# Moving unit 1.3's bonus work, a weight load and one r product in a hand-ordered RWKV-6 plus SwiGLU kernel

## The chip, the cores and the metric

The kernel runs on one core of a Trainium2 chip. The core has five instruction streams that run beside each other: TensorE (PE in the profile, with its weight loads listed as PEld), VectorE (DVE), ScalarE (ACT), GpSimd (POOL) and SyncE (SP), which here only issues DMAs. Each stream works through its instructions in the order in which the program issued them; a semaphore makes one wait for another. The metric is the device time of one execution in microseconds (us), lower is better.

## The reference

The first half is an RWKV-6 attention over 4 batches, 8 heads, 768 positions and a head size of 48; the second half a SwiGLU feed-forward on its output, 3072 tokens of width 384, hidden width 1536.

```
for t in range(S):
    cur = einsum('bhd,bhe->bhde', u[None] * kt, vt)
    y[:, :, t] = einsum('bhd,bhde->bhe', rt, state + cur)
    state = wt[:, :, :, None] * state + einsum('bhd,bhe->bhde', kt, vt)
x = y.transpose(0, 2, 1, 3).reshape(B * S, H * D)
xn = x / sqrt(mean(x * x) + 1e-6) * rms_g
g, val = xn @ w_gate, xn @ w_val
out = (g * sigmoid(g) * val) @ w_out
```

Inputs and output are float32; the kernel multiplies in bfloat16.

## The kernel before

**Tiling.** The sequence is cut into six blocks of 128 positions. A unit n.j is block n of batch j, so there are 24 units, and each has the same steps. Positions lie on the partitions. Inside a block the recurrence becomes matrix products: the decays are logged (ln), summed along the block by a triangular matmul (cs_mm) and exponentiated (exp_r, exp_k); r_mul and k_mul scale r and k with them; rk_pe and rk_tr bring both to head-major form (by TensorE transposes and a ScalarE copy in blocks 0 and 1, by a DMA transpose from block 2 on); q_mm gives the 128x128 products per head, q_mask_e and, after q_copy_o, q_mask_o keep their lower triangles (even and odd heads); y_mm multiplies them with v, and with the state carried from the block before; st_mm and st_new make the next state.

**The bonus term.** The diagonal, r·(u·k) times v, is a separate strand: bonus_mul (two GpSimd products, lines 467 and 468, into one of three buffers "ruk"), bonus_sum (a VectorE sum, line 472), bonus_v (a GpSimd product with v, line 477), and x_add on VectorE, which joins it to y. In block 0, x_pe joins it by a TensorE matmul instead.

**The feed-forward.** x_sq, x_rstd, xn_mul, xn_pe and xn_out normalise x, transpose it and apply the gain. When the four units of a block are there, gate_mm and val_mm run for twelve pieces f of the hidden width, each three matmuls of 128x512 (line 626); silu and h_mul join the two; o_mm sums the twelve pieces into one output tile (line 672), o_out copies it and out_dma writes it. The feed-forward of block n runs between the attention steps of block n+1.

**Weights.** W_gate and W_val come in two parts: load_gv.0.0 and load_gv.0.1 bring the first 512 columns of gate and val, load_gv.1.0 and load_gv.1.1 the remaining 1024, and load_wo brings W_out in three thirds (four of its twelve pieces each, so that the ninth matmul of an o_mm is the first to read the last third). All of them are issued from GpSimd's queue (lines 351 and 357) and converted to bfloat16 on the way; r, k, v and w come through SP's queue (lines 248 and 261).

**Order.** The order of all steps is written out as one list of 1086 names, ORDER; the last loop of the program calls them one after the other, and each engine keeps that order among its own instructions. Nothing else schedules. k_mul is on VectorE in blocks 0 and 1 and on GpSimd after that; in block 1 its inputs, and those of r_mul, are both in SBUF (tiles er and ek), and in block 0 one is in PSUM.

**PSUM.** Eight banks are in three rings: a (two, gate and cs_r), b (two, val and cs_k) and q (four, all else). `psum` gives the bank whose last use lies furthest back in ORDER; the profile names them ps_au, ps_av, ps_bu, ps_bv, ps_qu, ps_qv, ps_qx, ps_qz. Matmuls named warm, ahead of the feed-forward's start, have no reader.

```
rings = {"a": [[-2, 0], [-2, 1]], "b": [[-2, 0], [-2, 1]], "q": [[-2, 0], [-2, 1], [-2, 2], [-2, 3]]}
for step in ORDER.split():
    fn, n, j = step.split(".")
    fns[fn](int(n), int(j))
    at[0] += 1
```

Of the kernel before, what the change touches and what calls it, by code (L numbers as in the profile page):

```python
# [51 lines left out]
x_rstd.1.0 q_mask_e.1.3 q_copy_o.1.2 val_mm.0.8 silu.0.8 val_mm.0.11 y_mm.1.1 silu.0.10 q_mask_e.1.2 bonus_sum.1.2
q_mask_o.1.3 h_mul.0.8 x_add.1.1 y_mm.1.3 st_mm.1.2 load_v.2.1 ln.2.0 st_mm.1.3 q_mask_o.1.2 val_mm.0.10 y_mm.1.2
x_sq.1.1 xn_mul.1.0 bonus_v.1.2 cs_mm.2.0 x_add.1.3 x_sq.1.3 st_new.1.2 h_mul.0.11 ln.2.1 h_mul.0.10 x_add.1.2
cs_add.2.0 o_mm.0.0 o_out.0.0 x_rstd.1.1 x_sq.1.2 xn_pe.1.0 xn_out.1.0 xn_mul.1.1 exp_r.2.0 st_new.1.3 cs_mm.2.1
cs_add.2.1 x_rstd.1.2 load_r.2.3 r_mul.2.0 o_mm.0.2 xn_pe.1.1 xn_mul.1.2 xn_pe.1.2 x_rstd.1.3 o_mm.0.1 xn_mul.1.3
# [5 lines left out]
gate_mm.1.5 cast_v.2.0 k_mul.2.3 silu.1.5 rk_tr.2.2 val_mm.1.5 load_w.3.3 o_out.0.2 h_mul.1.1 gate_mm.1.3 gate_mm.1.0
val_mm.1.0 h_mul.1.5 o_out.0.3 silu.1.0 val_mm.1.6 q_mm.2.0 load_v.2.3 q_copy_o.2.0 silu.1.3 q_mask_o.2.0 gate_mm.1.2
st_mm.2.0 h_mul.1.0 val_mm.1.3 rk_tr.2.3 h_mul.1.6 load_w.3.1 load_w.3.0 gate_mm.1.10 val_mm.1.2 load_k.3.1
q_mask_e.2.1 silu.1.2 st_new.2.0 gate_mm.1.4 q_copy_o.2.1 cast_v.2.2 silu.1.4 q_mask_o.2.1 h_mul.1.3 q_mask_e.2.0
y_mm.2.1 y_mm.2.0 h_mul.1.2 st_mm.2.2 bonus_v.2.0 silu.1.10 x_add.2.1 x_add.2.0 gate_mm.1.9 val_mm.1.4 x_sq.2.1
gate_mm.1.8 val_mm.1.9 bonus_mul.2.3 st_new.2.2 out_dma.0.1 x_sq.2.0 h_mul.1.4 load_v.3.2 x_rstd.2.0 silu.1.9 silu.1.8
q_mm.2.2 bonus_sum.2.2 q_copy_o.2.2 h_mul.1.9 gate_mm.1.11 q_copy_o.2.3 out_dma.0.2 load_w.3.2 cast_v.2.3 bonus_v.2.2
bonus_sum.2.3 q_mask_o.2.3 st_mm.2.3 load_k.3.0 q_mask_o.2.2 q_mask_e.2.3 val_mm.1.11 q_mask_e.2.2 val_mm.1.10
bonus_v.2.3 y_mm.2.3 silu.1.11 y_mm.2.2 ln.3.0 h_mul.1.11 h_mul.1.10 x_rstd.2.1 x_add.2.2 ln.3.1 val_mm.1.8 ln.3.3  # L70
h_mul.1.8 cs_mm.3.0 load_r.3.0 x_sq.2.2 xn_mul.2.0 cast_v.3.2 cs_add.3.0 x_add.2.3 exp_k.3.0 x_sq.2.3 o_mm.1.0
cs_mm.3.1 xn_pe.2.0 exp_r.3.0 ln.3.2 x_rstd.2.2 o_mm.1.1 st_new.2.3 load_r.3.1 out_dma.0.3 w_tot.3.0 r_mul.3.0
xn_mul.2.1 k_mul.3.0 xn_mul.2.2 cs_add.3.1 exp_k.3.1 xn_pe.2.2 cs_mm.3.3 x_rstd.2.3 o_out.1.0 exp_r.3.1 bonus_mul.3.1
xn_out.2.2 xn_mul.2.3 o_mm.1.3 w_tot.3.1 xn_pe.2.3 o_out.1.1 cs_add.3.3 r_mul.3.1 load_k.3.2 load_r.3.3 xn_pe.2.1
xn_out.2.0 exp_r.3.3 exp_k.3.3 cs_mm.3.2 xn_out.2.3 o_mm.1.2 load_r.3.2 k_mul.3.1 w_tot.3.3 rk_tr.3.0 r_mul.3.3
cs_add.3.2 out_dma.1.0 xn_out.2.1 load_v.3.0 exp_r.3.2 gate_mm.2.5 exp_k.3.2 r_mul.3.2 w_tot.3.2 val_mm.2.0 gate_mm.2.0
bonus_mul.3.0 bonus_mul.3.2 k_mul.3.2 o_out.1.3 bonus_sum.3.0 silu.2.5 rk_tr.3.1 load_k.3.3 o_out.1.2 q_mm.3.0 silu.2.0
q_mask_e.3.0 val_mm.2.1 bonus_v.3.0 h_mul.2.0 gate_mm.2.1 load_w.4.1 load_v.3.1 load_k.4.3 st_mm.3.2 k_mul.3.3
q_copy_o.3.0 silu.2.1 rk_tr.3.2 load_v.4.0 rk_tr.3.3 val_mm.2.5 gate_mm.2.11 load_k.4.0 bonus_sum.3.1 cast_v.3.0
out_dma.1.1 load_v.3.3 load_w.5.2 q_mask_e.3.1 q_copy_o.3.1 gate_mm.2.2 silu.2.11 h_mul.2.5 val_mm.2.2 h_mul.2.1  # L80
load_w.4.0 gate_mm.2.3 load_v.4.1 silu.2.2 q_mask_o.3.0 cast_v.3.1 load_r.4.1 bonus_sum.3.2 h_mul.2.2 bonus_v.3.1
# [643 lines left out]
```

## Time and profile before

| what | value |
|---|---|
| time, median of 3 runs | 200.89 us (199.61, 200.89, 200.95) |
| profiled execution | span 199.4 us from first to last instruction; no other time of it is recorded |
| TensorE busy | 194.7 us |
| VectorE busy | 151.5 us |
| ScalarE busy | 137.1 us |
| GpSimd busy | 125.7 us |
| granted TensorE clock | 1.00 throughout |
| DMA traffic | 32.41 MB, 163 GB/s over the span |

A timeline row reads: start and length in us, engine, source line, operation, output tile <- input tiles, shape, count, and in brackets how long the engine had been idle and what released it. A TensorE row of several matmuls ends with the modelled end of the last one, so rows overlap. A DMA row gives the issue, the size and the us from issue to landing. The queue named q0 is GpSimd's, q1 is SP's.

### The profile page before, as it was taken

Reading aid. Unit: us, or ns where it says so; the run is one execution under the profiler, and the core shown is the slowest. Engines: PE = TensorE matmul, PEld = TensorE weight load, DVE = VectorE, ACT = ScalarE, POOL = GpSimd, SP = SyncE. Lnnn points to the kernel's source line nnn. Section 1 sums busy time; section 2 is a strip of 40 time slices with the busy share of each in tenths; the row PEclk is TensorE's granted clock in tenths of the full one; section 3 lists DMA queues with packets and bytes.
Section 4 is the critical chain, followed back from the end, with each engine's and each line's share of the span. In section 5 each row is a group of like instructions: output and inputs, shape, how many; then the busy total and the mean of one; then the engine's idle time right before and its main releaser. Section 6 shows DMA issues by size and latency. Waiting matters only on the chain.

```text
span 199.4 us, 4410 instructions
## 1 busy us (share of the span) xinstructions
PE 194.7 (98%) x1577; PEld 115.6 (58%) x1577; DVE 151.5 (76%) x290; ACT 137.1 (69%) x279; POOL 125.7 (63%) x184
## 2 busy tenths in 40 slices
...
GB/s 147 265 229 191 169 206 208 201 207 191 203 173 212 204 191 227 217 191 191 177 175 226 214 203 215 179 174 139 122 190 219 0 24 60 2 116 82 0 59 100
DMA packets 121566, 32.41 MB, mean 163 GB/s; under 512 B 116420, under 2 KB 120392, under 8 KB 121544
## 3 DMA queue, kind: packets, MB, share of 16 engines
...
q8 instruction: 12, 0.20, 0.4%
...
## 4 chain that ended last, share of the span: by engine, by line
PE 88%; DMA 5%; DVE 2%; POOL 2%; issue 1%; ACT 0%
PE ps_bu L626 12%; PE ps_av L626 12%; PE ps_au L626 11%; PE ps_bv L626 11%; PE ps_qu L672 7%; PE ps_qz L672 7%; DMA wg_sb<-in_moe_w_gate_dram 5%; PE ps_qx L672 5%; PE ps_qv L672 5%; PE ps_qz L502 1%; PE ps_qx L552 1%; PE ps_qv L502 1%; PE ps_qv L333 1%; PE ps_qu L285 1%; PE ps_qu L502 1%
## 5 line engine op out<-in xcount | busy, mean ns | idle before, releaser
L672 PEld LDWEIGHTS <-ht 128*128 128x128 bf16 x300 | 28.2, 98 | 16.6
L626 PEld LDWEIGHTS <-wg_sb 128*128 128x128 bf16 x216 | 23.1, 114 | 19.8 <-DMA wg_sb<-in_moe_w_gate_dram 0.9
L626 PEld LDWEIGHTS <-wv_sb 128*128 128x128 bf16 x216 | 23.0, 114 | 18.3
L658 DVE TENSOR_TENSOR ht<-ps_bv,sg 128x512 bf16<-128x512 f32 x35 | 24.0, 687 | 10.2 <-PE ps_bv L626 9.1
L658 DVE TENSOR_TENSOR ht<-ps_bu,sg 128x512 bf16<-128x512 f32 x37 | 25.4, 687 | 6.9 <-PE ps_bu L626 5.8
L235 ACT ACTIVATE sg<-ps_av 128x512 bf16<-128x512 f32 x37 | 22.0, 596 | 12.2 <-PE ps_av L626 11.6
L626 PE MATMUL ps_av<-xnt,wg_sb 128*128 128x512 bf16 x111 | 30.1, 380 | 0.0
L626 PE MATMUL ps_bu<-xnt,wv_sb 128*128 128x512 bf16 x111 | 30.1, 380 | 0.0
L626 PE MATMUL ps_au<-xnt,wg_sb 128*128 128x512 bf16 x105 | 28.5, 380 | 0.5 <-DMA wg_sb<-in_moe_w_gate_dram 0.5
L626 PE MATMUL ps_bv<-xnt,wv_sb 128*128 128x512 bf16 x105 | 28.5, 380 | 0.0
L235 ACT ACTIVATE sg<-ps_au 128x512 bf16<-128x512 f32 x35 | 21.0, 600 | 10.5 <-PE ps_au L626 8.7
L467 POOL TENSOR_TENSOR ruk<-rt,kt 128x384 f32<-128x384 f32 x24 | 24.0, 1001 | 6.1 <-DMA kt<-in_k_dram 5.2
L468 POOL TENSOR_TENSOR ruk<-ruk,u_bc 128x384 f32<-128x384 f32 x24 | 24.7, 1030 | 1.9
L520 POOL TENSOR_SCALAR_AFFINE_SELECT qts<-qts 128x512 bf16<-128x512 bf16 x20 | 12.8, 650 | 15.1 <-ACT qts L513 14.6
L477 POOL TENSOR_TENSOR ydiag<-vt,diag 128x384 f32<-128x384 f32 x24 | 20.2, 843 | 1.7 <-DVE diag L472 1.6
L461 POOL TENSOR_TENSOR rk<-kt,ek 128x384 bf16<-128x384 f32 x16 | 15.9, 1004 | 2.3 <-ACT ek L235 2.3
L672 PE MATMUL ps_qu<-wo_sb,ht 128*128 128x384 bf16 (+1 forms) x96 | 15.0, 306 | 0.0
L672 PE MATMUL ps_qz<-wo_sb,ht 128*128 128x384 bf16 x84 | 14.8, 326 | 0.0
L233 ACT ACT_TABLE_LOAD x10 | 12.8, 1283 | 1.8 <-PEq L709 1.6
L472 DVE TENSOR_REDUCE diag<-ruk 128x8 f32<-128x384 f32 x24 | 13.0, 543 | 0.2 <-POOL ruk L468 0.2
L235 ACT ACTIVATE lw<-wt 128x384 bf16<-128x384 f32 (+1 forms) x20 | 11.1, 577 | 2.6 <-DMA wt<-in_w_dram 2.6
L585 ACT ACTIVATE xn<-xb,rstd 128x384 bf16<-128x384 f32 x20 | 11.8, 603 | 0.8 <-POOL rstd L580 0.7
...
## 6 DMA issues: line engine op xcount, KB each, us to landing
rt<-in_r_dram SPq DMA_DIRECT2D x24, 192.0 KB, 4.0
kt<-in_k_dram SPq DMA_DIRECT2D x24, 192.0 KB, 4.2
vt<-in_v_dram SPq DMA_DIRECT2D x24, 192.0 KB, 4.0
out_dram<-ob SPq DMA_DIRECT2D x23, 192.0 KB, 2.3
wt<-in_w_dram SPq DMA_DIRECT2D x16, 192.0 KB, 4.0
wt<-in_w_dram SPq DMA_DIRECT2D x4, 384.0 KB, 4.4
wo_sb<-in_moe_w_out_dram POOLq DMA_DIRECT2D x3, 384.0 KB, 7.0
...
```

Of the source, the lines that this page charges most:

```text
L233: nc.scalar.preload_act_table_set(table_name)
L235: return nc.scalar.activation(**kw).ins
L461: eng.tensor_tensor(out=rk[:, n % 2, j, 1, :, 0:D], in0=inp["k", n, j], in1=bank["cs_k", n, j][:, 0:DM].rearrange("p (h d) -> p h d", h=H) ...
L467: nc.gpsimd.tensor_tensor(out=ruk[n, j], in0=inp["r", n, j], in1=inp["k", n, j], op=ALU.mult)
L468: nc.gpsimd.tensor_tensor(out=ruk[n, j], in0=ruk[n, j], in1=u_bc, op=ALU.mult)
L472: nc.vector.tensor_reduce(out=diag[n, j].rearrange("p h o -> p (h o)"), in_=ruk[n, j], axis=mybir.AxisListType.X, op=ALU.add)
L477: nc.gpsimd.tensor_tensor(out=ydiag[n, j], in0=inp["v", n, j], in1=diag[n, j].to_broadcast([128, H, D]), op=ALU.mult)
L520: nc.gpsimd.affine_select(out=qts[n, j][:, 1], in_=qts[n, j][:, 1], compare_op=ALU.is_gt, fill=0.0, base=0, pattern=[[0, NP], [1, 128]], c ...
L585: nc.scalar.activation(out=xn, in_=xb[n, j], func=AF.Copy, scale=rstd[n, j][:, 1, c:c + 1])
L626: nc.tensor.matmul(ps[:, cols], lhsT=units(ws, c, f), rhs=xnt[n][:, c, cols], start=(first and c == 0), stop=(c == KC - 1))
L658: nc.vector.tensor_tensor(out=ht[n][:, f, :], in0=bank.pop(("v", n, f)), in1=bank.pop(("sg", n, f)), op=ALU.mult)
L672: nc.tensor.matmul(ps[:, cols], lhsT=ht[n][:, f, b * L:(b + 1) * L], rhs=wo_sb[:, f, cols], start=(f == 0), stop=(f == FC - 1))
```

## The change

Only ORDER is changed; all 1086 steps are still there. Engine by engine, the moves are:

- GpSimd: load_gv.0.1 goes ahead of bonus_v.0.3 (it stood behind bonus_mul.1.0, directly ahead of load_gv.1.0); bonus_mul.1.3 goes behind q_mask_o.1.0 (it stood behind load_gv.1.1).
- VectorE: bonus_sum.0.3 goes ahead of q_mask_o.0.2; r_mul.1.1 goes behind xn_out.0.3 (it stood ahead of st_new.0.0 and r_mul.1.0), and st_new.0.3 goes there too, behind it; k_mul.1.3 goes behind q_mask_e.1.1, and bonus_sum.1.3 behind h_mul.0.6; w_tot.2.3 and r_mul.2.3 change places.
- TensorE: rk_pe.1.3 goes behind gate_mm.0.5 (it stood ahead of val_mm.0.6); rk_pe.1.2 goes ahead of gate_mm.0.4.
- SP: load_v.1.2 goes ahead of load_v.1.1.
- ScalarE: nothing moves.

With the order, `psum` gives ps_qu and ps_qv the other way round to a part of the tiles of ring q.

```diff
-load_r.1.3 load_k.1.3 load_r.1.2 load_k.1.2 r_mul.0.1 load_v.1.0 load_v.1.1 load_v.1.2 exp_k.0.0 bonus_mul.0.1
+load_r.1.3 load_k.1.3 load_r.1.2 load_k.1.2 r_mul.0.1 load_v.1.0 load_v.1.2 load_v.1.1 exp_k.0.0 bonus_mul.0.1
...
-q_mask_o.0.0 rk_pe.0.3 q_mask_e.0.0 q_mm.0.2 x_pe.0.0 x_sq.0.1 cast_v.0.3 rk_tr.0.3 q_mask_o.0.2 load_gv.0.0
-bonus_sum.0.3 q_mask_e.0.2 cs_mm.1.1 x_rstd.0.1 q_mm.0.3 warm.17.0 bonus_v.0.2 q_mask_o.0.3 y_mm.0.0 warm.25.0
-exp_r.1.1 load_w.2.3 x_pe.0.2 load_k.2.1 cast_v.0.2 bonus_v.0.3 warm.20.0 x_sq.0.0 y_mm.0.2 st_mm.0.0 warm.6.0
+q_mask_o.0.0 rk_pe.0.3 q_mask_e.0.0 q_mm.0.2 x_pe.0.0 x_sq.0.1 cast_v.0.3 rk_tr.0.3 bonus_sum.0.3 q_mask_o.0.2
+load_gv.0.0 q_mask_e.0.2 cs_mm.1.1 x_rstd.0.1 q_mm.0.3 warm.17.0 bonus_v.0.2 q_mask_o.0.3 y_mm.0.0 warm.25.0 exp_r.1.1
+load_w.2.3 x_pe.0.2 load_k.2.1 cast_v.0.2 load_gv.0.1 bonus_v.0.3 warm.20.0 x_sq.0.0 y_mm.0.2 st_mm.0.0 warm.6.0
...
-y_mm.0.3 exp_k.1.1 cs_mm.1.3 k_mul.1.0 xn_pe.0.1 warm.0.0 bonus_mul.1.0 load_gv.0.1 load_gv.1.0 x_rstd.0.2 warm.30.0
-x_sq.0.3 xn_mul.0.2 r_mul.1.1 st_new.0.0 xn_pe.0.0 r_mul.1.0 warm.14.0 x_rstd.0.3 warm.28.0 warm.33.0 xn_pe.0.2
-xn_out.0.1 bonus_mul.1.1 warm.11.0 xn_mul.0.3 exp_k.1.3 xn_out.0.0 st_mm.0.3 xn_out.0.2 st_mm.0.2 xn_pe.0.3 exp_r.1.3
-st_new.0.3 cs_mm.1.2 rk_pe.1.0 xn_out.0.3 k_mul.1.1 st_mm.0.1 st_new.0.1 k_mul.1.3 gate_mm.0.0 exp_r.1.2 bonus_sum.1.0
-exp_k.1.2 rk_pe.1.1 gate_mm.0.3 rk_tr.1.0 val_mm.0.0 silu.0.0 bonus_sum.1.1 load_gv.1.1 load_r.2.2 bonus_mul.1.3
-silu.0.3 val_mm.0.2 rk_tr.1.1 h_mul.0.0 gate_mm.0.2 st_new.0.2 silu.0.2 gate_mm.0.1 bonus_sum.1.3 val_mm.0.3
-gate_mm.0.9 silu.0.1 h_mul.0.2 val_mm.0.1 gate_mm.0.6 silu.0.9 r_mul.1.3 h_mul.0.3 q_mm.1.0 h_mul.0.1 silu.0.6
-q_mask_e.1.0 q_copy_o.1.0 q_mask_o.1.0 gate_mm.0.11 gate_mm.0.7 q_copy_o.1.1 silu.0.7 rk_pe.1.3 q_mask_e.1.1
-q_mask_o.1.1 r_mul.1.2 bonus_v.1.0 val_mm.0.6 val_mm.0.7 cast_v.1.0 k_mul.1.2 rk_tr.1.3 gate_mm.0.5 h_mul.0.6 y_mm.1.0
-load_wo.0.0 val_mm.0.9 silu.0.11 bonus_v.1.1 cast_v.1.2 load_wo.1.0 st_mm.1.0 cast_v.1.1 gate_mm.0.4 rk_pe.1.2
+y_mm.0.3 exp_k.1.1 cs_mm.1.3 k_mul.1.0 xn_pe.0.1 warm.0.0 bonus_mul.1.0 load_gv.1.0 x_rstd.0.2 warm.30.0 x_sq.0.3
+xn_mul.0.2 r_mul.1.0 st_new.0.0 xn_pe.0.0 warm.14.0 x_rstd.0.3 warm.28.0 warm.33.0 xn_pe.0.2 xn_out.0.1 bonus_mul.1.1
+warm.11.0 xn_mul.0.3 exp_k.1.3 xn_out.0.0 st_mm.0.3 xn_out.0.2 st_mm.0.2 xn_pe.0.3 exp_r.1.3 cs_mm.1.2 rk_pe.1.0
+xn_out.0.3 r_mul.1.1 st_new.0.3 k_mul.1.1 st_mm.0.1 st_new.0.1 gate_mm.0.0 exp_r.1.2 bonus_sum.1.0 exp_k.1.2 rk_pe.1.1
+gate_mm.0.3 rk_tr.1.0 val_mm.0.0 silu.0.0 bonus_sum.1.1 load_gv.1.1 load_r.2.2 silu.0.3 val_mm.0.2 rk_tr.1.1 h_mul.0.0
+gate_mm.0.2 st_new.0.2 silu.0.2 gate_mm.0.1 val_mm.0.3 gate_mm.0.9 silu.0.1 h_mul.0.2 val_mm.0.1 gate_mm.0.6 silu.0.9
+r_mul.1.3 h_mul.0.3 q_mm.1.0 h_mul.0.1 silu.0.6 q_mask_e.1.0 q_copy_o.1.0 q_mask_o.1.0 bonus_mul.1.3 gate_mm.0.11
+gate_mm.0.7 q_copy_o.1.1 silu.0.7 q_mask_e.1.1 k_mul.1.3 q_mask_o.1.1 r_mul.1.2 bonus_v.1.0 val_mm.0.6 val_mm.0.7
+k_mul.1.2 cast_v.1.0 gate_mm.0.5 rk_pe.1.3 rk_tr.1.3 h_mul.0.6 bonus_sum.1.3 y_mm.1.0 load_wo.0.0 val_mm.0.9 silu.0.11
+bonus_v.1.1 cast_v.1.2 load_wo.1.0 st_mm.1.0 cast_v.1.1 rk_pe.1.2 gate_mm.0.4 h_mul.0.7 st_mm.1.1 silu.0.5 val_mm.0.5
...
-val_mm.1.7 exp_k.2.2 load_k.2.3 st_mm.2.1 rk_tr.2.0 bonus_sum.2.0 r_mul.2.3 w_tot.2.3 gate_mm.1.1 load_v.2.2 st_new.2.1
+st_mm.2.1 rk_tr.2.0 bonus_sum.2.0 w_tot.2.3 r_mul.2.3 gate_mm.1.1 load_v.2.2 st_new.2.1 k_mul.2.2 silu.1.7
```

138 lines of the change are left out of this document (69 added, 69 removed).

## The prediction

> **What bounds the kernel now.** I read the page first, then the chain of waits in order of time, then each engine's timeline from 20 to 55 us, where the moved steps lie. Of the page, the busy shares and the head of the chain; of the stretches, one row (busy us and count of PE, PEld, DVE, ACT, POOL; clock; DMA share; GB/s):
>
> ```profile
> PE 194.7 (98%) x1577; PEld 115.6 (58%) x1577; DVE 151.5 (76%) x290; ACT 137.1 (69%) x279; POOL 125.7 (63%) x184
> PE 88%; DMA 5%; DVE 2%; POOL 2%; issue 1%; ACT 0%
> 37.00:198.00 161.00, 159.42 (x1291) 94.61 (x1291) 124.33 (x236) 109.43 (x223) 101.57 (x149) 1.00 0.73 155
> ```
>
> TensorE is the bound. From 37.0 us it is busy for 159.42 us, so up to 196.4 us without a hole, at clock 1.00. A new wait of TensorE behind 37 us is therefore paid in full, and a gain has to be made ahead of it. The DMA part of the chain, and TensorE's timeline ahead of 37 us:
>
> ```profile
> 25.85 0.61 POOL wv_sb L351
> ...
> 26.60 10.27 DMA wg_sb<-in_moe_w_gate_dram
> ```
> ```profile
> 28.87 0.32 PE L374 MATMUL ps_qx<-still 128*128 128x384 bf16 x1
> 29.35 0.33 PE L530 MATMUL ps_qu<-vb,rk 128*128 128x96 bf16 x4 [0.16 <-DVE xnt L607]
> 29.82 0.33 PE L596 MATMUL ps_qv<-ident,xn 128*128 128x128 bf16 x3
> ...
> 31.95 0.61 PE L484 MATMUL ps_qv<-ident,rk 128*128 128x128 bf16 x8
> ...
> 34.99 0.81 PE L626 MATMUL ps_av<-xnt,wg_sb 128*128 128x512 bf16 x3
> 35.63 0.81 PE L626 MATMUL ps_bv<-xnt,wv_sb 128*128 128x512 bf16 x3
> 36.92 0.84 PE L626 MATMUL ps_au<-xnt,wg_sb 128*128 128x512 bf16 x3 [0.47 <-DMA wg_sb<-in_moe_w_gate_dram]
> ```
>
> Three holes are there to be won. A 128x384 matmul lets the next one start 0.16 us after its own start (the twelve of 52.66, quoted below: 2.11 less the last one's 0.33, over eleven), so the successor of 28.87 could have started at 29.03; it started at 29.35, held by xn_out of unit 0.1 on VectorE. A group of three takes 0.65 us to the next one's start (34.99 to 35.63), so the one at 36.92 could have started at 36.28, had the second gate block been there: 0.64 us lost. And xn_pe of unit 0.3 (29.82) lost 0.13.
>
> **The change, front part.** VectorE and GpSimd around it (idle ahead of a row in brackets):
>
> ```profile
> 24.91 1.35 DVE L455 TENSOR_TENSOR rk<-rt,er 128x384 bf16<-128x384 f32 x1
> ...
> 26.66 2.18 DVE L455 TENSOR_TENSOR rk<-rt,er 128x384 bf16<-128x384 f32 x1
> 28.75 0.55 DVE L607 TENSOR_TENSOR xnt<-ps_qu,gT 128x384 bf16<-128x384 bf16 x1
> ...
> 30.61 0.54 DVE L607 TENSOR_TENSOR xnt<-ps_qv,gT 128x384 bf16<-128x384 bf16 x1
> 31.08 0.82 DVE L461 TENSOR_TENSOR rk<-kt,ek 128x384 bf16<-128x384 f32 x1
> ...
> 36.73 0.55 DVE L455 TENSOR_TENSOR rk<-rt,er 128x384 bf16<-128x384 f32 x1
> ```
> ```profile
> 22.65 0.83 POOL L477 TENSOR_TENSOR ydiag<-vt,diag 128x384 f32<-128x384 f32 x1 [1.02 <-DVE diag L472]
> ...
> 27.40 1.01 POOL L467 TENSOR_TENSOR ruk<-rt,kt 128x384 f32<-128x384 f32 x1
> ...
> 31.55 1.21 POOL L468 TENSOR_TENSOR ruk<-ruk,u_bc 128x384 f32<-128x384 f32 x1
> ```
>
> (1) load_gv.0.1 goes ahead of bonus_v.0.3, into the 1.02 us that GpSimd idled at 22.65; its issue was worth 0.75 (25.85 to 26.60), so it is hidden. bonus_sum.0.3, one step earlier on VectorE, keeps bonus_v.0.3 at 22.4 to 22.65. load_gv.1.0 loses that issue ahead of it and goes out at 25.3 to 25.85. With its 10.27 us it lands at 35.6 to 36.1; with the second block queued directly behind the first, earlier still. TensorE will want it at 36.1 (below), so the 0.64 us go.
>
> (2) An r_mul with both inputs in SBUF takes 0.55 us beside an idle GpSimd (36.73) and 2.18 us beside a busy one (26.66); it ended at 28.84, 0.43 after the GpSimd product of 27.40. The k_mul at 31.08 took 0.82, and the GpSimd product beside it, 31.55, 1.21 for about 1.0. So each holds the other. The Trainium skill, "SBUF — State Buffer", section "Who interferes with whom", says that of a VectorE instruction with two SBUF inputs and a GpSimd instruction that reads SBUF, the later one blocks until the first ends; the trace agrees, and by a split of bandwidth in its place the lock terms below would be near nothing.
>
> With r_mul.1.1 gone from here, xn_out.0.1 waits for TensorE's transposes alone. st_mm.0.3 starts at 29.03, xn_pe.0.3 at 29.37, xn_out.0.3 at 29.75 for 30.61. Behind it now stand r_mul.1.1, st_new.0.3 and k_mul.1.1, at a step of 0.47 each (30.61 to 31.08): k_mul.1.1 starts at 31.15 and ends at 31.7 beside an idle GpSimd, since bonus_mul.1.3 is gone from there. rk_pe.1.1 needs it and starts at 31.75 for 31.95. TensorE has a new stall of about 0.25 there; 0.20 is kept. From there 0.20 + 0.64 = **0.84 us earlier at 36.9**, and no more, since k_mul.1.1 is the limit.
>
> (3) What pays for the earlier weights are SP's loads. Queue packets and MB in 23 to 25 us (weights moving), 25.6 to 27.9 (none moving), 32 to 39 (the large block); ahead of them the landings of k of 1.1 (issued 20.09) and r of 1.3 (20.78):
>
> ```profile
> kt<-in_k_dram SPq DMA_DIRECT2D x1, 192.0 KB, 6.3
> ```
> ```profile
> rt<-in_r_dram SPq DMA_DIRECT2D x1, 192.0 KB, 6.5
> ```
> ```profile
> q0 software_dynamic: 301, 0.31, 90.6%
> q1 hardware_dynamic: 345, 0.07, 28.3%
> ```
> ```profile
> q1 hardware_dynamic: 2772, 0.52, 115.6%
> ```
> ```profile
> q0 software_dynamic: 647, 1.29, 97.2%
> q1 hardware_dynamic: 642, 0.12, 15.9%
> ```
>
> SP's queue moves 226 KB per us alone, 35 beside the small blocks and 17 beside the large one. The free stretch at 25.6 now belongs to the second block. k of 1.1 landed at 26.4; between nothing and 190 KB of it were left at 25.4, so it lands between 26.4 and some 33. I take 45 KB and 27.7, as its neighbour r of 1.3 landed at 27.3, 0.9 us (192 KB) later. bonus_mul.1.1 then starts at 27.7 for 27.40, which costs nothing; beyond 31 it would hold k_mul.1.1. r of 1.3 has 192 KB more to wait for. At 155 KB per us (0.31 MB in 2 us) the second block takes 2.5 us, at 184 the large one 4.3, and beside them SP moves 88 and 73 of the 237 KB. Some 75 are left at 32.2, so r lands between 33.5 (a gap in the weights' queue) and 37.5 (none). r_mul.1.3 wants it at 36.3, and h_mul.0.3 stands behind it, whose buffer the next silu on ScalarE uses, ahead of q_copy_o.1.0. Between 0 and 0.65 us; I take 0.25. That leaves **0.6 us won** where unit 1's masks begin.
>
> The Trainium skill, "DMA: Bandwidth & Descriptors", section "Queues, rings and completion order", says that each DMA engine goes round its queues packet by packet. The trace agrees: 647 packets against 642, at ten times the bytes. By equal bytes SP would not starve, and the 0.25 would be nothing.
>
> **The change, unit 1.3.** bonus_mul.1.3 leaves 30.46, behind which GpSimd idled for 7.48 us, and goes behind the first affine_select of 40.23. GpSimd, then the wait of TensorE for what it issues:
>
> ```profile
> 40.23 1.54 POOL L520 TENSOR_SCALAR_AFFINE_SELECT qts<-qts 128x512 bf16<-128x512 bf16 x2 [7.48 <-ACT qts L513]
> 41.75 1.12 POOL L477 TENSOR_TENSOR ydiag<-vt,diag 128x384 f32<-128x384 f32 x1
> 42.82 0.61 POOL L357 DMA_DIRECT2D wo_sb<-in_moe_w_out_dram  x1
> ...
> 44.85 1.01 POOL L467 TENSOR_TENSOR ruk<-rt,kt 128x384 f32<-128x384 f32 x1
> ...
> 46.88 0.59 POOL L357 DMA_DIRECT2D wo_sb<-in_moe_w_out_dram  x1
> ...
> 49.24 1.22 POOL L520 TENSOR_SCALAR_AFFINE_SELECT qts<-qts 128x512 bf16<-128x512 bf16 x2
> ```
> ```profile
> wo_sb<-in_moe_w_out_dram POOLq DMA_DIRECT2D x1, 384.0 KB, 7.0
> ```
> ```profile
> DMA to landing us min/median/max: 6.3/7.0/7.5
> ```
> ```profile
> 50.65 0.33 PE L549 MATMUL ps_qx<-st,rkT 128*128 128x96 bf16 x4
> ...
> 52.66 2.11 PE L672 MATMUL ps_qx<-wo_sb,ht 128*128 128x384 bf16 x12
> ```
>
> GpSimd has no bracket from 40.23 to 50.4: it is full there. A pair of products costs 44.85 to 46.88, 2.03 us. To this comes the lock: k_mul.1.3, r_mul.1.2 and k_mul.1.2 on VectorE now fall on four GpSimd instructions. Before, two such meetings stretched a pair of selects from 1.22 (49.24) to 1.54 and a product from 0.83 (22.65) to 1.12, 0.6 us together; three to four meetings give 0.9 to 1.2. I take 0.4 more (ends 0 and 0.9). So everything behind it on GpSimd is 2.43 us late, 1.83 with the 0.6 won.
>
> Who waits: the select for unit 1.3 ended at 49.87 (half of the pair at 49.24) and y_mm.1.3 read it at 50.65, 0.78 of slack; 1.05 us are paid there. The last third of W_out was issued at 46.88 and landed 7.0 later, at 53.88. o_mm.0.0's twelve matmuls start 0.16 apart, and the ninth, the first to read that third, at 53.95: slack 0.07. It is issued at 48.7, lands at 55.7, and the ninth matmul is 1.76 us late. The 1.05 are part of these, not added.
>
> VectorE hides beneath. It ran h_mul.0.6 for val_mm.0.9's bank:
>
> ```profile
> 42.23 0.69 DVE L658 TENSOR_TENSOR ht<-ps_bv,sg 128x512 bf16<-128x512 f32 x1
> ```
> ```profile
> 43.62 0.82 PE L626 MATMUL ps_bv<-xnt,wv_sb 128*128 128x512 bf16 x3
> ```
>
> With k_mul.1.3 and three lock waits ahead of it h_mul.0.6 ends near 44.3 for 42.92, and val_mm.0.9 would be 0.7 late, less than what GpSimd costs. rk_pe.1.3 goes behind three groups (1.95 us), and its copy on ScalarE stands ahead of silu.0.11; gate_mm.0.4, which takes that silu's bank, comes behind the delayed val_mm.0.9, which covers it; uncovered it would cost some 0.5, inside the same wait. Nothing: the order of load_v.1.2 and load_v.1.1 (their casts stand in that order), w_tot.2.3 ahead of r_mul.2.3 (both run anyway), and the exchanged PSUM names u and v (same ring, same number in use).
>
> **Sum.** −0.84 + 0.25 + 2.03 + 0.40 − 0.07 = **+1.8 us**, carried to the end: a span of 201.2 for 199.4. The profiled execution's own time is known by its span alone; the runs were 199.61 to 200.95, median 200.89, 1.5 over the span. I forecast 200.89 + 1.8 = 202.7.
>
> **Rivals.** (A) Faster: the front gain stays and GpSimd's delay is not felt, 200.89 − 0.84 = 200.05. It decides at the ninth matmul of o_mm.0.0: W_out's last third must land by 53.1, so the delay would have to vanish in the queue. For it: the thirds landed 6.3 to 7.5 us after their issues, the first (42.82) by 49.1 and the last by 53.9, 4.8 apart where the issues are 4.06 apart, so the last waits in the queue. Against: the first is issued behind bonus_mul.1.3 too. 0.11. (B) W_out catches up on an emptier queue, and y_mm.1.3 alone decides: −0.59 + 2.43 − 0.78 = +1.06, 201.95. 0.22. (C) The loads starve more: r of 1.3 at 37.5 and k of 1.1 near 31, so that the masks start 0.6 later than reckoned and the lock takes its 0.9: 1.8 + 0.4 + 0.5 = +2.7 or more, 203.6. 0.2. The forecast has 0.47, with its own range of 202.0 to 203.4.
>
> **Chances.** A measurement of this kernel can tell about 1% (2.0 us) from no change, so slower begins at 202.9: all of C and about 0.4 of the forecast, 0.39. Faster, below 198.9, is beyond A: 0.02. The range goes from A's time to beyond C's: 200.0 to 204.0.
>
> **What would show it.** Right: no DMA wait ahead of the gate group near 36; TensorE waiting 0.2 to 0.3 for VectorE's L461 ahead of the transposes near 31.7; GpSimd idle from about 30 to 39.5, then two products between the selects; the third W_out issue near 48.7; waits of TensorE for GpSimd's select near 50 and for wo_sb inside the first L672 group. Wrong: if bonus_mul.1.1 waits for k of 1.1 beyond 29, if val_mm.0.9 waits longer than y_mm.1.3, or if the third W_out load lands sooner after its issue than 6.3 us.

## The result and the profile after

The kernel after takes 202.07 us (median of 6 runs, 201.33 to 203.19) where the kernel before, on the same chip, takes 200.49 (6 runs, 199.61 to 200.95). The ratio is 1.0078, with a 95% interval of 1.0053 to 1.0104: 1.58 us slower, less than 1%. Every ratio here leaves out the runs that lie over 1.5% above the fastest of their kernel. The profiled execution of the kernel after took 202.02 us, its span 200.3.

The page of the kernel after, busy shares and head of the chain:

```profile
PE 191.7 (96%) x1557; PEld 114.1 (57%) x1577; DVE 151.2 (75%) x290; ACT 137.2 (69%) x279; POOL 125.2 (63%) x184
...
PE 71%; POOL 8%; issue 7%; SPq 6%; DMA 6%; ACT 0%; POOLq 0%
```

TensorE's share of the chain is 71% here and was 88% on the page of before, but this can't be laid to the change: a second profile of the kernel before (before_again, below) has 71% too. The busy time of TensorE can't be compared with before, because 20 of its matmul records are missing here (1557 matmuls beside 1577 weight loads). Its start times can. TensorE's timeline of the kernel after:

```profile
30.00 0.81 PE L626 MATMUL ps_au<-xnt,wg_sb 128*128 128x512 bf16 x2
30.65 0.70 PE L484 MATMUL ps_qu<-ident,rk 128*128 128x128 bf16 x8
...
34.42 0.81 PE L626 MATMUL ps_bv<-xnt,wv_sb 128*128 128x512 bf16 x3
35.80 0.84 PE L626 MATMUL ps_au<-xnt,wg_sb 128*128 128x512 bf16 x3 [0.57 <-DMA wg_sb<-in_moe_w_gate_dram]
...
39.09 0.81 PE L626 MATMUL ps_av<-xnt,wg_sb 128*128 128x512 bf16 x3
40.08 0.84 PE L626 MATMUL ps_bv<-xnt,wv_sb 128*128 128x512 bf16 x3 [0.17 <-DMA wv_sb<-in_moe_w_val_dram]
...
42.67 0.36 PE L552 MATMUL ps_qz<-vb,qts 128*128 128x48 bf16 x8
43.36 0.81 PE L626 MATMUL ps_bv<-xnt,wv_sb 128*128 128x512 bf16 x3 [0.33 <-DVE ht L658]
...
50.54 0.19 PE L552 MATMUL ps_qx<-vb,qts 128*128 128x48 bf16 x1
51.03 0.35 PE L552 MATMUL ps_qx<-vb,qts 128*128 128x48 bf16 x7 [0.30 <-POOL qts L520]
...
52.85 1.46 PE L672 MATMUL ps_qx<-wo_sb,ht 128*128 128x384 bf16 x8
54.81 0.81 PE L672 MATMUL ps_qx<-wo_sb,ht 128*128 128x384 bf16 x4 [0.50 <-DMA wo_sb<-in_moe_w_out_dram]
```

A bracket gives the idle time that the profile counts; from start to start the loss is a little more, since a pipelined successor would have started before its forerunner's modelled end. Three waits behind 42 us are new. Eight matmuls of 128x48 take about 0.20 to the next start, so val_mm.0.9 lost 0.49 at 43.36. One of them takes 0.02, so y_mm.1.3 lost 0.47 at 51.03. Eight of 128x384 take 1.30, so the ninth, due at 54.15, lost 0.66 at 54.81. Together 1.62 us, against 1.58 measured; the interval of the ratio, 1.06 to 2.08 us, is far wider than the 0.04 between them. Ahead of 42 us the wait for the large gate block is still there (34.42 to 35.80 is 0.73 more than the 0.65 of three matmuls), and a wait for the large val block has come (0.34 by the same count, at 40.08). This one comes with the move of rk_pe.1.3, which no longer stands ahead of val_mm.0.6: all eight profiles of kernels with that move show it (brackets of 0.17 to 0.23 us), and none of the six without it.

GpSimd and VectorE of the kernel after, two rows of the front and then the stretch where the loss arises, and the landing of the third W_out load:

```profile
26.40 0.80 POOL L351 DMA_DIRECT2D wg_sb<-in_moe_w_gate_dram  x1
27.23 1.01 POOL L467 TENSOR_TENSOR ruk<-rt,kt 128x384 f32<-128x384 f32 x1
...
39.12 0.63 POOL L520 TENSOR_SCALAR_AFFINE_SELECT qts<-qts 128x512 bf16<-128x512 bf16 x1 [9.07 <-ACT qts L513]
39.73 1.29 POOL L467 TENSOR_TENSOR ruk<-rt,kt 128x384 f32<-128x384 f32 x1
41.10 1.19 POOL L468 TENSOR_TENSOR ruk<-ruk,u_bc 128x384 f32<-128x384 f32 x1
42.25 0.95 POOL L520 TENSOR_SCALAR_AFFINE_SELECT qts<-qts 128x512 bf16<-128x512 bf16 x1
43.17 0.83 POOL L477 TENSOR_TENSOR ydiag<-vt,diag 128x384 f32<-128x384 f32 x1
43.95 0.61 POOL L357 DMA_DIRECT2D wo_sb<-in_moe_w_out_dram  x1
...
47.99 0.59 POOL L357 DMA_DIRECT2D wo_sb<-in_moe_w_out_dram  x1
...
50.35 1.22 POOL L520 TENSOR_SCALAR_AFFINE_SELECT qts<-qts 128x512 bf16<-128x512 bf16 x2
```
```profile
35.49 0.55 DVE L455 TENSOR_TENSOR rk<-rt,er 128x384 bf16<-128x384 f32 x1
...
39.51 0.66 DVE L461 TENSOR_TENSOR rk<-kt,ek 128x384 bf16<-128x384 f32 x1
40.09 1.35 DVE L455 TENSOR_TENSOR rk<-rt,er 128x384 bf16<-128x384 f32 x1
41.36 1.35 DVE L461 TENSOR_TENSOR rk<-kt,ek 128x384 bf16<-128x384 f32 x1
42.63 0.68 DVE L658 TENSOR_TENSOR ht<-ps_bv,sg 128x512 bf16<-128x512 f32 x1
```
```profile
wo_sb<-in_moe_w_out_dram POOLq DMA_DIRECT2D x1, 384.0 KB, 6.8
```

From the first select to the third W_out issue GpSimd needs 8.87 us (39.12 to 47.99) where it needed 6.65 before (40.23 to 46.88): 2.22 more. The two products stand at 39.73 and 41.10, beside two VectorE products stretched to 1.35.

### The profile page after: what moved, and what is told of

It is laid out like the page before. It is cut to its first block, busy times and chain, and to the rows that moved or that the text cites. A ratio compares the mean times of both kernels' runs of the same rounds, so it can differ in the third digit from the quotient of the medians.

```text
span 200.3 us, 4388 instructions
## 1 busy us (share of the span) xinstructions
PE 191.7 (96%) x1557; PEld 114.1 (57%) x1577; DVE 151.2 (75%) x290; ACT 137.2 (69%) x279; POOL 125.2 (63%) x184
## 4 chain that ended last, share of the span: by engine, by line
PE 71%; POOL 8%; issue 7%; SPq 6%; DMA 6%; ACT 0%; POOLq 0%
PE ps_av L626 10%; PE ps_bu L626 10%; PE ps_bv L626 9%; PE ps_au L626 9%; PE ps_qv L672 7%; PE ps_qz L672 7%; PE ps_qu L672 5%; PE ps_qx L672 4%; SPq L248 4%; DMA wo_sb<-in_moe_w_out_dram 3%; POOL ruk L467 3%; DMA rt<-in_r_dram 2%; SPq L261 2%; POOL ruk L468 2%; POOL ydiag L477 1%
## 5 line engine op out<-in xcount | busy, mean ns | idle before, releaser
L626 PE MATMUL ps_bu<-xnt,wv_sb 128*128 128x512 bf16 x103 | 29.3, 380 | 0.5
L672 PE MATMUL ps_qv<-wo_sb,ht 128*128 128x384 bf16 (+1 forms) x96 | 15.0, 306 | 0.0
L235 ACT ACTIVATE lw<-wt 128x384 bf16<-128x384 f32 (+1 forms) x20 | 11.1, 579 | 4.2 <-DMA wt<-in_w_dram 4.2
L570 ACT ACTIVATE junk<-xb 128x384 bf16<-128x384 f32 x20 | 10.4, 522 | 2.8 <-DVE xb L561 2.6
```

What stands on the lines that cost most here:

```text
L235: return nc.scalar.activation(**kw).ins
L570: nc.scalar.activation(out=junk, in_=xb[n, j], func=AF.Square, accum_out=rstd[n, j][:, 0, c:c + 1])
L626: nc.tensor.matmul(ps[:, cols], lhsT=units(ws, c, f), rhs=xnt[n][:, c, cols], start=(first and c == 0), stop=(c == KC - 1))
L672: nc.tensor.matmul(ps[:, cols], lhsT=ht[n][:, f, b * L:(b + 1) * L], rhs=wo_sb[:, f, cols], start=(f == 0), stop=(f == FC - 1))
```

## The experiments

Two theories stood at the start. One: the whole loss comes from the place of bonus_mul.1.3 on GpSimd, and the front part wins something beside it. The other: the front part wins nothing, or costs. The first four kernels ran together (kernel before 200.18 us, 23 runs), the next four too (200.5, 23 runs), then three (200.23, 24 runs) and one (200.77, 17 runs).

**bonus_back.** The kernel after with bonus_mul.1.3 alone put back.

```diff
-load_gv.1.1 load_r.2.2 silu.0.3
+load_gv.1.1 bonus_mul.1.3 load_r.2.2 silu.0.3
...
-q_mask_o.1.0 bonus_mul.1.3 gate_mm.0.11
+q_mask_o.1.0 gate_mm.0.11
```

> The changed kernel with bonus_mul.1.3 alone put back behind load_gv.1.1, into GpSimd's idle stretch. Theory (the loss is GpSimd's 2.0 to 2.4 us behind q_mask_o.1.0, paid at W_out's last third): the loss goes and the front gain of 0.6 to 0.8 us stays, so about 199.8 us for 200.5 before, ratio 0.995 to 0.998; the third W_out issue near 46.0 and no wait for it on TensorE. Rival (the loss comes from the earlier weight load that starves SP's loads): it stays near 202.0, ratio 1.007.

Measured: 200.55 us, ratio 1.0019 (0.9995 to 1.0043). The three new waits are gone from its trace; those for the gate and val blocks stay:

```profile
35.70 0.84 PE L626 MATMUL ps_au<-xnt,wg_sb 128*128 128x512 bf16 x3 [0.86 <-DMA wg_sb<-in_moe_w_gate_dram]
...
39.98 0.84 PE L626 MATMUL ps_bv<-xnt,wv_sb 128*128 128x512 bf16 x3 [0.18 <-DMA wv_sb<-in_moe_w_val_dram]
```

So this one step carries the three waits and with them 1.2 us of the 1.6 by the ratios. What is left lies within the interval, 0.1 us won to 0.9 lost; the wait for the val block, 0.33 us there from start to start, may be part of it.

**unit13_only.** The kernel before with the four steps of unit 1.3 moved (and rk_tr.1.3 behind rk_pe.1.3) and nothing else.

```diff
-st_new.0.1 k_mul.1.3 gate_mm.0.0
+st_new.0.1 gate_mm.0.0
...
-load_gv.1.1 load_r.2.2 bonus_mul.1.3 silu.0.3
+load_gv.1.1 load_r.2.2 silu.0.3
...
-gate_mm.0.1 bonus_sum.1.3 val_mm.0.3
+gate_mm.0.1 val_mm.0.3
...
-q_mask_o.1.0 gate_mm.0.11 gate_mm.0.7 q_copy_o.1.1 silu.0.7 rk_pe.1.3 q_mask_e.1.1
+q_mask_o.1.0 bonus_mul.1.3 gate_mm.0.11 gate_mm.0.7 q_copy_o.1.1 silu.0.7 q_mask_e.1.1 k_mul.1.3
...
-k_mul.1.2 rk_tr.1.3 gate_mm.0.5 h_mul.0.6 y_mm.1.0
+k_mul.1.2 gate_mm.0.5 rk_pe.1.3 rk_tr.1.3 h_mul.0.6 bonus_sum.1.3 y_mm.1.0
```

> The kernel before with the moves of unit 1.3 alone (bonus_mul, k_mul, bonus_sum, rk_pe and its copy rk_tr behind it). Theory: GpSimd late by 2.2 us without the front gain to set against it, 200.5 + 2.1 = 202.6 us, ratio 1.010 to 1.012, with the wait for W_out's last third inside the first output tile. Rival (front is the cause): 200.5 us, ratio 0.999 to 1.001.

Measured: 202.51 us, ratio 1.0106 (1.0071 to 1.014), which is 2.1 us more. The same three waits stand in its trace (brackets 0.30, 0.20 and 0.37 at 43.96, 51.63 and 55.28). Its interval overlaps that of the kernel after, so whether the front part takes back anything of it can't be said from this.

**front_only.** The kernel after with the four steps of unit 1.3 where they were.

```diff
-st_mm.0.1 st_new.0.1 gate_mm.0.0
+st_mm.0.1 st_new.0.1 k_mul.1.3 gate_mm.0.0
...
-load_gv.1.1 load_r.2.2 silu.0.3
+load_gv.1.1 bonus_mul.1.3 load_r.2.2 silu.0.3
...
-gate_mm.0.2 st_new.0.2 silu.0.2
+gate_mm.0.2 st_new.0.2 bonus_sum.1.3 silu.0.2
...
-q_mask_o.1.0 bonus_mul.1.3 gate_mm.0.11
+q_mask_o.1.0 gate_mm.0.11
...
-q_mask_e.1.1 k_mul.1.3 q_mask_o.1.1 r_mul.1.2 bonus_v.1.0 val_mm.0.6
+q_mask_e.1.1 q_mask_o.1.1 r_mul.1.2 bonus_v.1.0 rk_pe.1.3 val_mm.0.6
...
-gate_mm.0.5 rk_pe.1.3 rk_tr.1.3 h_mul.0.6 bonus_sum.1.3 y_mm.1.0
+gate_mm.0.5 rk_tr.1.3 h_mul.0.6 y_mm.1.0
```

> The changed kernel with all four steps of unit 1.3 where they were; the weight load, r_mul.1.1, bonus_sum.0.3 and the rest moved. Theory: the front gain alone, 0.6 to 0.8 us, so 199.7 to 199.9 us, ratio 0.996. Rival (front is the cause of the loss): 202.0 us.

Measured: 200.27 us, ratio 1.0006 (0.9981 to 1.003). The front part is worth nothing that this measurement can see, between 0.4 us won and 0.6 lost; 0.6 to 0.8 won was expected. Its trace still has the wait for the gate block (a bracket of 0.61 at 35.51).

**before_again.** The kernel before, unchanged, for a second look at its start.

> The kernel before itself, for a second profile of it and its time beside its span. Theory: its span and what its runs show are the same as in the first profile, 199.4 us, with the second gate block landing near 36.9 us. Rival: executions differ in the first 37 us by up to 1 us, with the landing of the loads on SP's queue, so that the first profile was a slower execution than the median one and the front gain reckoned from it, 0.84 us, is too large; then the span is 198.4 to 198.9 us.

Measured: 199.68 us, span 197.9. The head of its chain, then its VectorE, GpSimd and TensorE at the start:

```profile
PE 71%; DMA 10%; SPq 6%; POOL 6%; issue 3%; ACT 2%; DVE 0%; POOLq 0%
```
```profile
25.67 0.88 DVE L455 TENSOR_TENSOR rk<-rt,er 128x384 bf16<-128x384 f32 x1
```
```profile
21.01 1.62 POOL L477 TENSOR_TENSOR ydiag<-vt,diag 128x384 f32<-128x384 f32 x2
...
25.62 0.77 POOL L351 DMA_DIRECT2D wg_sb<-in_moe_w_gate_dram  x1
```
```profile
29.19 0.81 PE L626 MATMUL ps_au<-xnt,wg_sb 128*128 128x512 bf16 x2
29.84 0.39 PE L484 MATMUL ps_qv<-ident,rk 128*128 128x128 bf16 x4
30.74 0.40 PE L484 MATMUL ps_qv<-ident,rk 128*128 128x128 bf16 x4 [0.52 <-DVE rk L461]
...
34.21 0.81 PE L626 MATMUL ps_bv<-xnt,wv_sb 128*128 128x512 bf16 x3
35.12 0.84 PE L626 MATMUL ps_au<-xnt,wg_sb 128*128 128x512 bf16 x3
```

Three rows on which the prediction's front part rested are different in this execution of the same program. GpSimd doesn't idle ahead of bonus_v.0.3 (two of them run as one row at 21.01; it idled 1.02 us before), r_mul.1.1 takes 0.88 us (2.18 before), and the large gate block is issued at 25.62 (26.60 before). The feed-forward starts at 29.19 (31.30 before). The idle time of GpSimd isn't a peculiarity of the first profile, though: unit13_only, whose order is the same up to there, has it again, and so has gv_pair below (1.02 us at 22.72).

```profile
22.66 0.83 POOL L477 TENSOR_TENSOR ydiag<-vt,diag 128x384 f32<-128x384 f32 x1 [1.02 <-DVE diag L472]
```

What is left to win in before_again is 0.26 ahead of the gate group (34.21 to 35.12, less 0.65) and 0.68 at rk_pe.1.1.

**gv_alone** and **r_alone.** The kernel before with one part of the front each: load_gv.0.1 moved, or r_mul.1.1 and st_new.0.3 moved.

```diff
-load_w.2.3 x_pe.0.2 load_k.2.1 cast_v.0.2 bonus_v.0.3
+load_w.2.3 x_pe.0.2 load_k.2.1 cast_v.0.2 load_gv.0.1 bonus_v.0.3
```
```diff
-cs_mm.1.2 rk_pe.1.0 xn_out.0.3 k_mul.1.1
+cs_mm.1.2 rk_pe.1.0 xn_out.0.3 r_mul.1.1 st_new.0.3 k_mul.1.1
```

> The kernel before with load_gv.0.1 alone moved ahead of bonus_v.0.3. Theory (prediction, step 1): the second gate block lands 0.8 to 1.3 us earlier and the 0.64 us wait for it goes, 0.64 us faster, ratio 0.997. Rival (GpSimd has no idle time there in most executions, the block's issue moves little): ratio 0.999 to 1.001.

> The kernel before with r_mul.1.1 (and st_new.0.3 behind it) alone moved behind xn_out.0.3. Theory: the feed-forward starts about 1 us earlier, and TensorE waits that much longer for the second gate block, whose landing does not depend on it: ratio 0.999 to 1.001. Rival (the start itself is what is worth having): 0.5 to 1 us faster, ratio 0.995 to 0.998.

Measured: gv_alone 200.54 us, ratio 0.9991 (0.9966 to 1.0016); r_alone 200.76, ratio 1.003 (1.001 to 1.005), which is 0.2 to 1.0 us slower where no change was expected. In gv_alone GpSimd has no idle time to hide the issue in (VectorE's bonus_sum.0.3 ended at 21.61, the issue is at 22.71), and the large gate block is issued at 26.88. In r_alone VectorE's r_mul.1.1 meets bonus_mul.1.3 in its old place, and TensorE's rk_pe.1.1 waits twice for what stands behind it:

```profile
28.93 2.08 DVE L455 TENSOR_TENSOR rk<-rt,er 128x384 bf16<-128x384 f32 x1
```
```profile
31.54 0.38 PE L484 MATMUL ps_qu<-ident,rk 128*128 128x128 bf16 x4 [1.20 <-DVE st L537]
32.34 0.40 PE L484 MATMUL ps_qu<-ident,rk 128*128 128x128 bf16 x4 [0.42 <-DVE rk L461]
```

In this execution the moved r product costs more than it saves. It isn't the place of bonus_mul.1.3 alone: front_only and bonus_back have it there too, but it waited for k, started at 30.92 and 30.91 (29.58 here), and r_mul.1.1 took 0.64 and 0.63 us. No run shows that the move pays.

**gate_early** and **gv_pair.** Is it the issue of the large gate block that keeps the front gain away? The first is bonus_back with load_gv.1.0 ahead of bonus_mul.1.0, the second the kernel before with load_gv.0.1 and load_gv.1.0 there.

```diff
-warm.0.0 bonus_mul.1.0 load_gv.1.0 x_rstd.0.2
+warm.0.0 load_gv.1.0 bonus_mul.1.0 x_rstd.0.2
```
```diff
-warm.0.0 bonus_mul.1.0 load_gv.0.1 load_gv.1.0 x_rstd.0.2
+warm.0.0 load_gv.0.1 load_gv.1.0 bonus_mul.1.0 x_rstd.0.2
```

> The kernel after with bonus_mul.1.3 back behind load_gv.1.1 (200.55 when it ran), and in addition load_gv.1.0 ahead of bonus_mul.1.0, so that the large gate block is issued near 23.8 us instead of 26.25. Theory: the front gain was not won because the issue of the large gate block hardly moved (GpSimd had no idle time there to hide load_gv.0.1 in), so TensorE still waited 0.86 us for it near 35.7. Then that wait is gone or below 0.3 here, the block lands at or before 34.5, and the time is 199.6 to 200.1, 0.4 to 0.9 below the kernel before's fast runs less nothing. Rival: SP's loads pay for it; k and r of units 1.1 and 1.3 land 1 to 3 us later, VectorE's products and with them the transposes of TensorE wait 0.5 to 2 us near 31 to 33, and the time is 200.6 to 202.5.

> The kernel before with load_gv.0.1 and load_gv.1.0 both ahead of bonus_mul.1.0 and nothing else: both issues 2.2 us earlier, the large gate block near 24.2. Theory (issue decides): no wait for the gate block near 36, 199.4 to 200.0. Rival (SP's loads pay): waits for k or r between 29 and 33, 200.5 to 202.5.

Measured: gate_early 199.99 us, ratio 1.0001 (0.9971 to 1.003). Its TensorE has no wait for the gate block, as the theory said: the block was issued at 23.75 and landed 10.8 later, at 34.55, where TensorE came to it at 34.66. Its row of that group has no bracket:

```profile
34.66 0.81 PE L626 MATMUL ps_au<-xnt,wg_sb 128*128 128x512 bf16 x3
```

But no gain over the kernel before is measured, between 0.6 us won and 0.6 lost. SP's loads do pay, as the rival said, but not where it said: the waits are on GpSimd, and TensorE has no wait of 0.5 us for VectorE's products near 31 to 33. Beside bonus_back it takes 0.4 us less by the ratios, with intervals that overlap, so whether taking the wait away is worth anything stays open. Its GpSimd:

```profile
34.57 1.00 POOL L467 TENSOR_TENSOR ruk<-rt,kt 128x384 f32<-128x384 f32 x1 [5.13 <-DMA kt<-in_k_dram]
...
40.74 0.83 POOL L477 TENSOR_TENSOR ydiag<-vt,diag 128x384 f32<-128x384 f32 x1 [1.25 <-DMA vt<-in_v_dram]
```

In gv_pair seven of the twelve runs took 199.25 to 200.52 us and the other five 202.45 to 206.93. Its ratio, 0.9985 (0.9953 to 1.0017), is that of the seven and shows no change. Its profile is of one of the five, a run of 202.70 us, with a k product on VectorE that waits 3.38 us for k (35.06). Why these five are longer isn't shown: none of the seven was profiled. So gv_pair doesn't decide between theory and rival.

**third_product.** The kernel after with a third GpSimd product in bonus_mul.1.3; it multiplies the bonus of unit 1.3 by u twice.

```diff
         nc.gpsimd.tensor_tensor(out=ruk[n, j], in0=ruk[n, j], in1=u_bc, op=ALU.mult)
+        if (n, j) == (1, 3):
+            nc.gpsimd.tensor_tensor(out=ruk[n, j], in0=ruk[n, j], in1=u_bc, op=ALU.mult)
```

> The changed kernel with a third GpSimd product in bonus_mul.1.3 (unit 1.3's bonus is multiplied by u twice, so its output differs there). Theory: GpSimd is on the path behind q_mask_o.1.0, so one product of 1.0 us more, with up to 0.4 us of waiting for VectorE, comes out at the end one for one: 202.07 + 1.0 to 1.4 = 203.1 to 203.5 us, ratio 1.013 to 1.017. Rival (GpSimd is late but hidden): 202.1 us, ratio 1.008.

Measured: 202.56 us, ratio 1.012 (1.0091 to 1.0149). That is 0.5 us more than the kernel after by the times and 0.8 by the ratios, whose intervals overlap; 1.0 to 1.4 was expected. GpSimd was a full 0.97 later at the third W_out issue (48.94, which is 9.84 us behind the first select), but that load landed 6.4 us after its issue, 0.4 sooner than in the kernel after:

```profile
wo_sb<-in_moe_w_out_dram POOLq DMA_DIRECT2D x1, 384.0 KB, 6.4
```

TensorE left the first output tile 0.60 later (16.94 us behind the first select, for 16.34). Here part of the delay on GpSimd was given back by the queue.

**wo_early.** The kernel after with all three W_out loads ahead of bonus_mul.1.3, which takes the products out of W_out's way.

```diff
-q_copy_o.1.0 q_mask_o.1.0 bonus_mul.1.3
+q_copy_o.1.0 q_mask_o.1.0 load_wo.0.0 load_wo.1.0 load_wo.2.0 bonus_mul.1.3
```

> The changed kernel with the three W_out loads issued together behind q_mask_o.1.0, ahead of bonus_mul.1.3. Theory: the wait for W_out (0.67 us on TensorE in the profile of the changed kernel) goes; the wait of y_mm.1.3 for GpSimd's select (0.47 us there) stays or grows, since three issues of 0.6 us do not change the sum ahead of that select. The time falls by about 0.6 us from the changed kernel, 201.4 us, ratio 1.003 to 1.005. Rival (the earlier W_out takes the queues from v of unit 1 and the casts on ScalarE wait): no gain, 202.0 us or more.

Measured: 207.48 us (six runs, 204.69 to 208.64), ratio 1.0268 (1.0221 to 1.0315): 5.4 us worse than the kernel before, and by the ratios 3.8 worse than the kernel after. Between 41 and 48 us W_out moves 1.12 MB and SP's queue, with the v of unit 1, only 0.24. The v load that TensorE waits for lands 9.63 us after it got its turn; TensorE stands still for it, and after that its matmuls of 128x512 start 0.43 apart instead of 0.22. The wait on TensorE, the piece of the chain ahead of it, and a stretch behind it with its granted clock (the number behind the busy times):

```profile
48.64 0.33 PE L530 MATMUL ps_qv<-vb,rk 128*128 128x96 bf16 x4 [3.33 <-ACT vb L379]
49.83 1.48 PE L626 MATMUL ps_av<-xnt,wg_sb 128*128 128x512 bf16 x3
51.11 1.48 PE L626 MATMUL ps_bv<-xnt,wv_sb 128*128 128x512 bf16 x3
```
```profile
38.42 9.63 DMA vt<-in_v_dram
```
```profile
48.60:52.20 3.60, 3.56 (x13) 1.27 (x12) 1.72 (x3) 2.90 (x6) 3.33 (x5) 0.56 0.98 197
```

**wo_third** and **wo_two_first.** Which of GpSimd's two late products, the third W_out load or the select of unit 1.3, is paid? The first kernel issues only the third load 2.0 us sooner; the second puts bonus_mul.1.3 behind the first two W_out issues and ahead of the third (bonus_sum.1.3 goes behind st_new.1.1). Both are edits of the kernel after.

```diff
-h_mul.0.9 cast_v.1.3 gate_mm.0.10 bonus_mul.1.2 val_mm.0.4 st_new.1.0 st_new.1.1 load_wo.2.0
+h_mul.0.9 cast_v.1.3 gate_mm.0.10 load_wo.2.0 bonus_mul.1.2 val_mm.0.4 st_new.1.0 st_new.1.1
```
```diff
-q_mask_o.1.0 bonus_mul.1.3 gate_mm.0.11
+q_mask_o.1.0 gate_mm.0.11
...
-bonus_v.1.1 cast_v.1.2 load_wo.1.0 st_mm.1.0
+bonus_v.1.1 cast_v.1.2 load_wo.1.0 bonus_mul.1.3 st_mm.1.0
```

> The kernel after with the last third of W_out issued ahead of bonus_mul.1.2 instead of behind it, 2.0 us earlier, near 46.0; nothing else. Theory: the third W_out load and the select of unit 1.3 share the loss; the wait of 0.66 us inside the first L672 group goes, the wait of 0.3 us for the select stays or grows by 0.3 (bonus_mul.1.2 and the select keep their time), so 201.3 to 201.8. Rival 1: the landing is set by the queue and not by the issue, the wait stays, 202.0 to 202.2. Rival 2: the earlier transfer takes the queues from the v of unit 1, as it did when all three thirds were early, 202.5 or more.

> The kernel after with bonus_mul.1.3 behind load_wo.1.0, that is behind the first two W_out issues and still ahead of the third, and bonus_sum.1.3 behind st_new.1.1; nothing else. GpSimd has done the same work when it comes to the third issue and to the select of unit 1.3, so these are as late as in the kernel after (48.0 and near 50); only the first two W_out issues are 2.2 us earlier. Theory (the first W_out issue starts a transfer of 1.15 MB that the queues take some 10.8 us for, whatever the order of the issues inside it): the wait for W_out inside the first L672 group is below 0.2 us, the wait of 0.2 to 0.6 for the select stays, the wait of 0.33 for the ht product is gone, 200.7 to 201.4. Rival (each third lands some 6.8 us after its own issue): the wait for W_out stays at 0.5 or more, 201.6 to 202.2.

Measured: wo_third 201.35 us, ratio 1.0088 (1.0054 to 1.0122), no better than the kernel after by ratio; wo_two_first 202.02 us, ratio 1.0065 (1.0034 to 1.0096), not told apart from it either. TensorE of wo_third, then of wo_two_first, and the third load's landing in the latter:

```profile
52.05 1.46 PE L672 MATMUL ps_qx<-wo_sb,ht 128*128 128x384 bf16 x8
54.10 0.81 PE L672 MATMUL ps_qx<-wo_sb,ht 128*128 128x384 bf16 x4 [0.58 <-DMA wo_sb<-in_moe_w_out_dram]
```
```profile
50.73 0.19 PE L552 MATMUL ps_qx<-vb,qts 128*128 128x48 bf16 x1
51.80 0.35 PE L552 MATMUL ps_qx<-vb,qts 128*128 128x48 bf16 x7 [0.89 <-POOL qts L520]
...
53.62 2.11 PE L672 MATMUL ps_qx<-wo_sb,ht 128*128 128x384 bf16 x12
```
```profile
wo_sb<-in_moe_w_out_dram POOLq DMA_DIRECT2D x1, 384.0 KB, 5.5
```

In wo_third the wait for W_out stays (0.75 from start to start), although the third load was issued 2.0 us sooner: its first rival holds. From the first W_out issue (43.23) to the ninth matmul's release (54.10) it takes 10.87 us there, and 10.84 from the first issue to the landing in the kernel after (43.95 to 47.99 and 6.8 more), with third issues 2.0 and 4.04 us behind the first. So the issue of the first third is what counts, and a third issue up to 4 us behind it is made up for. wo_two_first says the same from the other side: the first issue is early again (42.57, which is 3.09 us behind the first select for 4.83), the third even later than in the kernel after (9.28 us behind the first select), it lands 5.5 us after its issue and the wait is gone. The making up has an end there: the third issue is 6.19 us behind the first, and the landing 11.69. The wait of val_mm.0.9 is gone too, with no GpSimd product beside VectorE's any more. But the select's wait grew from 0.47 to 1.05 us (50.73 to 51.80, less 0.02): counted from the first select, TensorE came to it 0.17 sooner, and GpSimd, which had waited 0.77 for v, finished it 0.41 later. Two things are late on GpSimd, and where one of them is freed, TensorE meets the other.

## Why the prediction was right, and where not

The forecast was 202.7 us with a range of 200.0 to 204.0, a loss of 1.8 us; measured are 202.07 and 1.58. Of the 0.6 between the times, 0.2 is the loss and 0.4 the median of three runs, 200.89, which was high (200.49 with six). The total was right, and partly by luck: of its terms one failed and the others were too large, and the two errors cancel. The front part with its loads was reckoned at −0.59 and nothing of it was measured; the part on GpSimd was reckoned at 2.36, and the three waits come to 1.62.

**The front part, −0.84: failed.** The step that failed is (1), that load_gv.0.1 is hidden in an idle stretch of GpSimd, that load_gv.1.0 goes out at 25.3 to 25.85, and that the wait for the gate block goes. The issue was at 26.40 in the kernel after, and the wait was 0.73, not nothing. Moving load_gv.0.1 did not bring the block's issue forward. It is at 25.62 to 26.61 in the four profiles that have both loads in their old places (the two of the kernel before, unit13_only and r_alone), and at 26.04 to 27.01 in the eight that have load_gv.0.1 alone moved.

Behind it stands a wrong reading of the base: one execution was taken for all. The prediction took a span of 199.4 to belong to a run of about 200.89, "1.5 over the span". In the later runs time less span is 1.7 to 1.8 (202.02 to 200.3, 199.68 to 197.9), so that the first execution took about 201.1, more than any of the three runs given. The 2.18 us of r_mul.1.1 are in no other profile with its old place (0.88 to 1.15 there). The 1.02 us of idle time on GpSimd are in some executions (the first profile, unit13_only, gv_pair) and not in others (before_again, r_alone), where VectorE had come to bonus_sum.0.3 at 20.13 and 20.66 for 22.03; what makes them differ isn't shown. In none of the profiles with load_gv.0.1 moved did the issue find such a stretch: bonus_sum.0.3 had always ended before it. What the move is worth in an execution that has the stretch stays open. What front_only measures in place of −0.84 is +0.1, with an interval of −0.4 to +0.6. gate_early shows that the wait could be taken away by an issue 2.5 us sooner, and that no gain over the kernel before is measured even then.

Of step (2) the order of events was right. r_mul.1.1 took 0.55 us (29.41) and k_mul.1.1 started 1.40 us behind xn_out.0.3 (30.34 and 28.94), just as reckoned (31.15 and 29.75). The new stall at rk_pe.1.1 was 0.09 (0.70 for the eight transposes, where 0.61 is usual), not 0.2 to 0.3.

**r of 1.3, +0.25: nothing.** r_mul.1.3 ran at 35.49 in the kernel after and waited for no DMA. bonus_mul.1.1 started at 27.23, directly behind the issue ahead of it, so k of 1.1 was not late either. The starving that step (3) describes shows where weights are earlier still: GpSimd waits 5.13 us for k in gate_early, and a v load takes 9.63 in wo_early. For the change as made it was overrated.

**GpSimd, 2.03 + 0.40 − 0.07: right in kind, 0.4 too large.** The products are between the selects and GpSimd is 2.22 us late at the third issue, for 2.43. Of the difference, the lock terms account: the two products took 2.52 instead of 2.03, but bonus_v.1.0 behind them only 0.78 to the next start instead of 1.07, so the lock cost 0.20 and not 0.40. The Trainium skill, "SBUF — State Buffer", section "Who interferes with whom", says that a VectorE instruction with two SBUF inputs contends with a GpSimd instruction that reads SBUF. This trace agrees again: VectorE's 0.55 became 1.35 twice here and 2.08 in r_alone. The landing was 6.8 us after the issue for 7.0. Less that and the slack of 0.07, 1.95 is left, and TensorE's ninth matmul was 1.96 late: 1.62 in the three waits and 0.34 already spent in the new wait for the val block at 40.08, which covered that much of GpSimd's delay. The prediction put the move of rk_pe.1.3 at nothing and didn't have this wait.

**How it shares out: the places right, the shares not.** The prediction had val_mm.0.9 late by 0.7 and covered (0.49), y_mm.1.3 paying 1.05 (0.47), and the ninth matmul of o_mm.0.0 the rest (0.66). The waits stand at these three places. One of its signs of being wrong came true by a hair, since val_mm.0.9 waited longer than y_mm.1.3 (0.49 and 0.47). That first wait is VectorE's: h_mul.0.6 (42.63) stands behind the products stretched to 1.35. Its word that the last third waits in the queue behind the first was the better explanation of W_out: up to a third issue some 4 us behind, it is the first issue that sets the landing, and the sum, which counted the third issue, came out the same only because both are late by the same 2.2 us.

**The rivals.** (A) fell: the delay didn't vanish in the queue, the ninth matmul waited. (B), 201.95, is near the measured time, but not by its mechanism, since W_out did not catch up; in wo_two_first the wait for W_out is gone and the select's wait is what is paid, at a ratio of 1.0065. (C) fell with the loads.
